# Token-shift features of a two-block layer: gelu output written at the commonest shift, seven shift copies per chunk for twelve, and a new written-out order

## The chip, the cores and the metric

The kernel runs on one core of a Trainium2 chip. The metric is the device time of one execution in microseconds (us); "before" has a median of 192.87 us over 6 runs (192.69 to 193.13). A core has five instruction streams that the kernel fills: TensorE (PE, matrix products; its weight loads are shown as PEld), VectorE (DVE), ScalarE (ACT), GpSimd (POOL) and SyncE (SP), which here only issues DMA transfers. Each takes its instructions strictly in order; they wait for each other through semaphores.

## The reference

The input x is 2048 rows of 448 features; weights and data are bf16.

```python
# A: attention block, 16 heads of 28 features, 8 keys at distance 0, 2, ... 14 rows back
qkv = (layernorm(x) @ wqkv)
attn = softmax(q . k * 28**-0.5 over the 8 keys, keys before row 0 masked)
h = x + (attn @ v) @ wo
# B: token shift and MLP, c = 112
y = layernorm(h)                              # B's own input
g = gelu(layernorm(y) @ w1)
g0 = rows of g[:, 0:112]   moved down by 1    # row s takes row s-1, row 0 takes zeros
g1 = rows of g[:, 112:224] moved up by 1      # row s takes row s+1
g2 = rows of g[:, 224:336] moved down by 2
g3 = rows of g[:, 336:448] moved up by 2
x1 = y + concat(g0, g1, g2, g3) @ w2
out = h + x1 + gelu(layernorm(x1) @ w3) @ w4  # w3 448x1792, w4 1792x448
```

## The kernel before

**Tiling.** The rows are cut into 4 chunks (c = 0 to 3) of 512. Inside a chunk even rows (p = 0) and odd rows (p = 1) are kept apart, 256 each, so that a shift by an even number of rows stays in its half and a shift by one row changes the half. A tile is 128 rows of one parity, and there are 16 of them (`NTL`). Features lie on partitions for the products: 448 features are read as four windows of 128 (`windows`).

**Operations.** `_fast_path` builds a list of operations, each with a tag, an engine, and the operations that it depends on. The tags, which this text uses as names (c a chunk, g a group of tiles):

- A1_c: layer norm of x, statistics on DVE, the factors on POOL, the normalised tiles `lntm` on ACT or DVE, and the transposes into `hT`: by PE for chunks 0 and 1 (four 128x128 transposes per tile into PSUM, then a copy to `hT` on ACT or DVE), by DMA from SP for chunks 2 and 3, one per tile (tr2_0 to tr2_3, tr3_0 to tr3_3).
- V_c, QK_c: products with wqkv; their .e0 to .e3 copy PSUM to `vt` and `qk`, on ACT or DVE.
- S_c.p, E_c.p, AV_c.p: scores (p is one of two groups of heads), exponential on ACT with a mask product on DVE, and the product with v. N_c is the division by the softmax sum, for chunks 2 and 3 with transfers through DRAM (zg, zs, zb).
- WO_c: product with wo; its .e0 and .e1 add x on DVE.
- B1_c, X_c, W1_c: layer norms of B (transposed by one DMA, tr1, tr2 or tr0, into `actT`), and the product with w1, whose .e0 and .e1 are the gelus.
- G_c: the shift copies. W2_g: the product with w2. L3_g, W3_g, W4_g: layer norm, w3 with gelu, w4. W2 to W4 work on groups of tiles (`GROUPS`: 2, 4, 4, 4 and 2), since a chunk's last rows need the next chunk's features.

**Shifts.** Each of the four feature groups has 112 features: 64 (window 0 of the gelu result `gA`), 32 and 16. Features 0 to 63 of all groups sit in `gA`, in two windows, one for each parity, and the shift there is only a choice of columns in `g_rows`. The remaining 48 features per group are packed in three 128-partition slots: two slots with the 32-feature blocks (both parities), one slot with 16-feature blocks, in which both parities stand on different partitions. The gelu .e1 writes these 768 columns to `gtm` (128x768), and G_c copies them from there to `gB` (four copies of 32x512) and `gC` (eight copies of 32x256 and 16x256) at the wanted shift. In the last chunk three small memsets fill columns at the end. `shift` lets a copy run on ACT or DVE, as the order says. `w1_p` is w1 with its columns repacked to make the features come out on those partitions, and `w2_s` is w2 with its rows in the same order; `load_attn_out` does both.

**What sets the order.** Nothing is decided at run time. `_ORDER` is a written table of operation numbers. A letter behind a number (a, v, p) chooses ACT, DVE or POOL, and digits behind a colon name PSUM banks. `schedule` fills the engines' queues in that order, `_emit_plan` adds the semaphore waits, `emit` (L1390) issues them; most instructions carry L1407, so tiles' names tell them apart. The figures `occ` and `lat` in the code describe durations to the program that wrote the table; they reach the chip only through it.

**Start.** PE first runs `WARM` products on zeros. `START` is the offset in instructions, within blocks of 256, at which PE's stream begins.

**Loads.** All weights are loaded by SP: wqkv first, then w1, w2 and wo. The w3 halves (w300, w301, w310, w311, 448 KB each) and w4 (w40 to w43) follow in four or more places in the middle. Each has no dependency, so its place in SP's queue alone decides when it starts.

Of the kernel before, what the change touches and what calls it, by code (L numbers as in the profile page):

```python
# [228 lines left out]
WARM = 14  # L229
LATE = 2  # L230

START = 128
# [3 lines left out]
2 1 4 3 7 6 8 5 12 17 0 16 13 15 45 65 74 64 67 68 79 21 19 18:7 22 20 28 23 24 25 26 29 27 35 30 32 36:7 33:6  # L236
31 38 39:5 37a 41 34a 42:7 40v 43v 51:40 52 53 14 59 84 82 48v 156 47v 9 10 50a 62 63 80 49a 46a 78 69 134 132
72 73 138 136 135 139 133 137 11 178 142 54 180 85:62 71 86 87 88 184 205 185 140 182 70 179 98 99 101 103 102
113 109 111 110 106 107 104 112 108 105 57a 141 56a 97 89a 100 91:40 90a 92 220:26 93 201 181 143 221 223 144v
153v 150v 183 94 145:3 146a 147v 55:2 95a 96v 151:7 154:6 58v 148:3 152v 149v 203 76 75 77 222 224 188 155a  # L240
234:40 186 187 166:62 237 238 123p 167 168 204 60 235 236 61 225:54 198 165 115a 230 226 231 227 232 228 233 229
170a 169 171a 172:60 189 196a 173 174 175 197 239:54 161:3 240 244 241 245 242 246 243 247 66 130 190a 191 176a
177a 164a 346:06 382 192a 193 199 200 206 202 207 209 81 349 347 194v 157:42 158 159 117p 119v 160 348 208 162a
248:06 249 250 350 163a 360:24 252 251 361 254 253 210 213a 378:1 351:32 381a 363 362 255 356 260 364 256 121a
258 257 259 261 195 264 215a 389:60 352 390 214 118a 391 211a 217a 393a 262 365:54 370 366 371 367 372 368 369
218 263 392 394a 353 265 269v 267v 124 357 266a 383:26 354 535:04 538 373 536 219 384 385 386 355 388a 358 114p
268v 359 537 374:04 375 376 120v 387a 377 128 539 379a 116p 380a 528:26 416:04 529 417 270 418 531 419 540:6 530
216 532 126 420 421 403 424 122p 428 426 422 425 429 427 423 279:02 430 432 212 541a 543 125 431 280 281 282
533:6 283 534v 284 433 434v 437v 293a 294a 295a 439 436v 129 286v 288v 291v 292v 289v 440 404:04 435a 287a 405
406 407 296a 409a 542 408a 438 290a 273 271 272 274 544 441 395:62 396 397 398 285v 401v 400a 276v 278v 275v  # L250
277v 297:04 298 299 300 301 302 303 304 305 306 442 545 443a 549 446v 546 447:26 448 449 451 307 308 309 310 450
452 456v 459v 463v 454v 461a 457a 453v 462v 460a 458a 464a 445v 410:40 411 412 414a 455v 547 413 548 415v 131
312v 399:7 311v 402a 552 465:24 551 666:60 313 550 466 467 553 667 469 669 468 470 473 554:60 555 556 558 477
474 478 316:42 317 318 557 319 475 559 44 320 471 476 472 560 127 562 566 563 564 561 322:46 323 324 325 567 565
481 479 480 482 570 568 569 571 484v 579 483v 321 486v 328:02 577 578 314 329 330 331 327 326 334:46 335 670 332
336 333 668 338 337 485a 315 673:02 572v 340:5 487 339 343:7 676 574v 575a 573v 576 671:2 341 674 677 675 678:0
344 672v 489 490 492:64 493 494 488 495 491 680 679a 681 682 683 684 685 687 497 496 342 686 580 583v 585:02 586
587 588 589 590 599v 600a 595v 596v 592a 498:64 591v 594v 499 500 501 601a 593v 503 504:20 505 506 507 602a 597v
598v 581v 502 508 444v 603:64 604 605 607 83 609 611 509 610 688 510:02 511 512 513 689 612 606 608 691 613 514
615 690 616 614 515 617 516:7 519:6 692:42 693 694 695 517 520 618 518 619 620 623v 624v 621v 622a 625 627 521  # L260
697 696 704 698 700 701 699 705 702 703 706 707 708 525:7 744 522:6 629 745 526 523 709 713a 642:42 643 644 710v
712a 711v 524 714 717 626 527 645 584v 630:60 631 632 633 647 715 716 718 646 635 634 636:42 637 582v 638 640
746 639 641 723:60 724 725 648:24 649 650 727 652 726 728 722v 719v 732a 720v 736v 733v 735a 739v 730v 741a 734
731v 729v 742 738a 743a 740v 651 653 737 654:7 812:02 813 814 721v 815 655 816 817 820 345 818 821 819 749:64
750 751 752 824 753 754 757 656 755 758 822 823 825 756 759 761 762 760 765 747:3 628 663:2 763 764 660:7 826a
827a 828 664 766 748 661 662 770a 769v 768v 767v 657:6 849:24 850 851 852 771 658 831:60 832 833 854 853 835
837:24 834 836 838 839 840 843:06 844 845 842 841 829 846 848 830 847 782:24 783 784 788:06 786 785 787 789 790
791 792 793 665 776:42 777 778 780 794:60 795 796 797 779 781 799 858:5 659 774 806:4 855:3 859 856 857 860 798
772 775 800:7 807 773 801 802 808 803:6 809:7 804 805 810 811
""".split()  # L270


def _fast_path(nc, es, flag, A_x, A_wqkv, A_wo, B_w1, B_w2, B_w3, B_w4, out):
    SEQ, D = A_x.shape[1], A_x.shape[2]
# [14 lines left out]
    def sb(name, shape, dt):  # L289
        return es.enter_context(nc.sbuf_tensor(name, shape, dt))  # L290
# [1208 lines left out]
```

## Time and profile before

| | |
|---|---|
| median of 6 runs | 192.87 us |
| profiled execution | 193.29 us, span 191.6 us, granted clock 1.00 |
| PE's first warm-up product, first V_0 product | 2.58 us, 8.46 us |
| first statistics on DVE | 3.62 us |
| AV_2.0 starts | 59.73 us |
| S_3.0 starts, W3_0 starts | 77.68 us, 82.85 us |
| instruction transfers (queue q8) | 25 of 16 KB |

The span runs from the first instruction of the profiled execution to the last. The page gives, for each engine, its busy time; then the chain that ended last (each piece followed back to what released it), the costliest groups of instructions (busy time and mean duration in ns, then the idle time ahead of the group and who ended it), and the DMA queues. An idle time attributed to "issue" is one for which the profile shows no producer. A timeline row gives start, length, engine, operation, tiles and count, and in brackets the idle time ahead. DMA rows for a stretch give queue and kind, packets, MB, and time taken as a share of the stretch times 16 transfer engines.

### The profile page before, as it was taken

How to read it: one execution, taken by the hardware profiler on the slowest of the kernel's cores; microseconds unless marked ns; L12 is line 12 of the kernel's file. 1: busy time of each engine (PE TensorE's matmuls, PEld its weight loads, DVE VectorE, ACT ScalarE, POOL GpSimd, SP SyncE). 2: the span in 40 equal slices, each digit the busy share in tenths (PEclk: the TensorE clock that was granted, in tenths of full speed). 3: DMA queues.
4: the chain of work that ended last, by engine and by line, in shares of the span. 5: the costliest groups of instructions: out<-in, count | busy, mean ns of one | idle time of the engine just before them, and what ended most of it. 6: DMA issues, size and time to landing. Idle time of an engine off the chain costs nothing.

```text
span 191.6 us, 6790 instructions
## 1 busy us (share of the span) xinstructions
PE 183.1 (96%) x2999; PEld 102.3 (53%) x2999; DVE 128.8 (67%) x313; ACT 112.1 (59%) x149; POOL 41.3 (22%) x101
## 2 busy tenths in 40 slices
PE   7999999998897999999999999999999999999994
PEld 2445556554555564577556464444566568454551
DVE  7899988999985779999773379794038970001241
ACT  2769899597849749938758930117782326564000
POOL 3147400507104603005910002143000320000000
DMA  5975307437297766620653600507000133000021
GB/s 141 337 241 139 94 12 153 34 33 145 92 144 217 196 159 151 71 88 0 113 119 91 163 3 0 129 28 182 2 0 27 41 98 104 3 0 3 3 99 51
DMA packets 32479, 17.77 MB, mean 93 GB/s; under 512 B 22524, under 2 KB 31932, under 8 KB 32444
## 3 DMA queue, kind: packets, MB, share of 16 engines
q1 hardware_dynamic: 32156, 17.05, 37.8%
q8 instruction: 25, 0.41, 0.9%
q10 hardware_dynamic: 288, 0.23, 0.4%
q14 instruction: 10, 0.08, 0.2%
HBM read 10.07 MB, written 1.90 MB: 62 GB/s over the span
## 4 chain that ended last, share of the span: by engine, by line
PE 78%; ACT 9%; DVE 8%; POOL 2%; DMA 1%; issue 1%
PE ps L1407 78%; DVE st L1407 3%; ACT gC L1407 2%; POOL rstd L1407 2%; DMA xin<-in_A_x_dram 1%; ACT gtm L1407 1%; DVE xin L1407 1%; ACT gA L1407 1%; ACT qk L1407 1%; ACT pt L1407 1%; ACT vt L1407 1%; DVE qk L1407 1%; DVE lntm L1407 1%; DVE xb L1407 1%; DVE mv L1407 1%
## 5 line engine op out<-in xcount | busy, mean ns | idle before, releaser
L1407 PE MATMUL ps<-actT,w_s 64*128 64x512 bf16 (+2 forms) x560 | 44.2, 312 | 0.0
L1407 PE MATMUL ps<-w_s,arena 128*128 128x448 bf16 x224 | 43.4, 353 | 0.0
L1407 DVE TENSOR_TENSOR xb<-ps,xb 128x448 bf16<-128x448 f32 (+1 forms) x26 | 18.4, 724 | 32.8 <-PE ps L1407 32.7
L1407 ACT ACTIVATE arena<-ps 128x512 bf16<-128x512 f32 (+2 forms) x40 | 29.0, 767 | 16.9 <-PE ps L1407 16.6
L1407 PEld LDWEIGHTS ps<-actT,w_s 64*128 64x128 bf16 x560 | 26.3, 94 | 16.9 <-DVE xb L1407 0.4
L1407 PEld LDWEIGHTS ps<-w_s,arena 128*128 128x128 bf16 x224 | 21.4, 98 | 20.8 <-ACT arena L1407 0.6
L1407 PE MATMUL ps<-hT,arena 64*128 64x512 bf16 x224 | 25.7, 377 | 0.1
L1407 POOL TENSOR_TENSOR rstd<-vtmp,mhalf 128x4 f32<-128x4 f32 (+1 forms) x16 | 18.4, 1153 | 1.1
L1407 DVE BATCH_NORM_STATS2 st<-xin 128x6 f32<-128x448 bf16 x32 | 18.1, 605 | 0.2 <-DMA xin<-in_A_x_dram 0.2
L1407 ACT ACTIVATE pt<-ps 128x1024 bf16<-128x1024 f32 x16 | 15.7, 1021 | 3.6 <-PE ps L1407 3.5
L1407 PEld LDWEIGHTS ps<-hT,arena 64*128 64x128 bf16 x224 | 10.8, 94 | 11.6 <-ACT qk L1407 0.4
L1407 ACT ACTIVATE qk<-ps 128x1024 bf16<-128x1024 f32 x14 | 13.9, 1021 | 2.9 <-PE ps L1407 2.8
L1407 ACT ACTIVATE lntm<-xin,nmr,rstd 128x512 bf16<-128x512 bf16 x13 | 10.2, 808 | 8.8 <-POOL nmr L1407 8.3
L1407 PE MATMUL ps<-arena,hT 64*64 64x448 bf16 (+1 forms) x248 | 15.1, 352 | 0.2 <-DVE hT L1407 0.2
L1407 POOL TENSOR_SCALAR vtmp<-mv 128x4 f32<-128x4 f32 (+1 forms) x16 | 3.4, 215 | 50.0 <-DVE mv L1407 49.2
L1407 PE MATMUL ps<-wo_s,oT 64*128 64x448 bf16 x128 | 13.1, 350 | 0.6 <-ACT vt L1407 0.5
L1407 POOL TENSOR_SCALAR nmr<-mv 128x4 f32<-128x4 f32 (+1 forms) x16 | 4.3, 272 | 41.9 <-DVE mv L1407 41.8
L1407 PE MATMUL ps<-actT,w_p 64*128 64x512 bf16 (+1 forms) x140 | 13.0, 333 | 0.0
L1407 ACT ACTIVATE lntm<-xb,nmr,rstd 128x512 bf16<-128x512 bf16 x5 | 4.0, 812 | 15.1 <-POOL nmr L1407 15.1
L1407 DVE COPY gC<-gtm 32x256 bf16<-32x256 bf16 (+1 forms) x15 | 3.4, 228 | 13.3 <-ACT gtm L1407 12.9
L1407 DVE TENSOR_TENSOR pt<-pt,msk 128x1024 bf16<-128x1024 bf16 x16 | 10.5, 683 | 0.7 <-ACT pt L1407 0.7
L1407 PEld LDWEIGHTS ps<-actT,w_p 64*128 64x128 bf16 x140 | 8.4, 94 | 3.9
(90 smaller groups left out, 226.3 us busy)
## 6 DMA issues: line engine op xcount, KB each, us to landing
w_s<-in_B_w_dram SPq DMA_DIRECT2D x6, 448.0 KB, 4.2
rzb<-rz_scratch SPq DMA_DIRECT2D x8, 256.0 KB, 4.4
out_dram<-xb SPq DMA_DIRECT2D x16, 112.0 KB, 2.1
xin<-in_A_x_dram SPq DMA_DIRECT2D x3, 448.0 KB, 7.2
arena<-in_A_wqkv_dram SPq DMA_DIRECT2D x2, 448.0 KB, 5.6
w_s<-in_B_w_dram SPq DMA_DIRECT2D x2, 336.0 KB, 5.1
arena<-in_A_wqkv_dram SPq DMA_DIRECT2D x2, 224.0 KB, 4.9
w_s<-in_B_w_dram SPq DMA_DIRECT2D x2, 224.0 KB, 3.6
```

The lines of the kernel that those rows point to most:

```text
L1407: inst = getattr(eng, meth)(**kw)
```

## The change

Three things are changed.

*The shift copies.* `gtm`, `gB` and `gC` become one tile `gBC` of four slots (128 partitions, 4 x (HALF+4) columns). The gelu .e1 writes slots 0 to 2 directly at an offset of 2, so a feature whose shift is the one that this offset gives needs no copy. Of the two 32-feature slots only partitions 32 to 63 (by 1) and 96 to 127 (by 2) are moved, in place, to the left. Slot 3 is a moved image of slot 2: a copy of all 128 partitions, then four copies of 32 or 16 partitions over parts of it. That is seven copies per chunk, and no memsets in the last one. The 16-feature blocks are put on other partitions (the constants in `load_attn_out`, for `w2_s` and `w1_p`), so that blocks of one shift lie side by side.

*The order.* `_ORDER` is new throughout, with other engine letters. PE's operations keep nearly the same sequence. The numbers of operations change by one to six, as there are fewer of them. Of the places spoken of below: the four copies that empty the first transposes (A1_0) run on ACT, ACT, DVE, DVE (tiles 1, 0, 2, 3) before, and tiles 0 and 2 on ACT, 1 and 3 on DVE after; the normalise for tr2_0 moves behind V_1's evictions on ACT; in SP's queue, w300 and w40 before V_2, then tr2, tr3_2, w310, tr3_0, zg1, w301, w41 become w40, tr3_2, tr2, tr3_1, tr3_0, w301, w300, w41, zg1, and w310 and w311 stand behind the zb transfers of chunk 2. The engines of the shift copies after (ACT + DVE) are 2 + 5, 2 + 5, 1 + 6 and 2 + 5 for chunks 0 to 3.

*Small constants.* One warm-up product fewer, another start offset (128 becomes 132), wv loaded ahead of wqk, and figures in the cost model, which act only through the order.

```diff
-WARM = 14
+WARM = 13
 LATE = 2
-START = 128
+START = 132
 _ORDER = """
...
-31 38 39:5 37a 41 34a 42:7 40v 43v 51:40 52 53 14 59 84 82 48v 156 47v 9 10 50a 62 63 80 49a 46a 78 69 134 132
...
+2 17 1 59 3 4 5 6 8 7 82 0 64 16 12 21 15 19 22 20 28 23 24 25 26 13 67 68 18:7 29 35 27 30 36:7 32 31 33:6 34a
+38 14 41 9 10 11 39:5 37v 42:4 43v 79 111 69 40a 65 50a 49v 48v 47a 72 74 155 45 46v 78 133 135 51:60 131 137 52
...
-    gB = sb("gB", [128, 2, HALF + 4], BF16)
-    gC = sb("gC", [128, HALF + 4], BF16)
-    gtm = sb("gtm", [128, 2, 768], BF16)
+    gBC = sb("gBC", [128, 4, HALF + 4], BF16)
...
-    win_load("wqk", wqk_s, A_wqkv[:, 0:2 * D], 512 * 2 * D * 2, ("sp", "sp"))
-    win_load("wv", wv_s, A_wqkv[:, 2 * D:3 * D], 512 * D * 2, ("sp", "sp"))
+    win_load("wv", wv_s, A_wqkv[:, 2 * D:3 * D], 512 * D * 2, ("sp", "sp"), 190.0)
+    win_load("wqk", wqk_s, A_wqkv[:, 0:2 * D], 512 * 2 * D * 2, ("sp", "sp"), 280.0)
...
-        pool("memset", 140, ap=gB[:, :, 0:2], constant=0.0)
-        pool("memset", 140, ap=gB[:, :, HALF:HALF + 2], constant=0.0)
-        pool("memset", 140, ap=gC[:, 0:2], constant=0.0)
+        pool("memset", 140, ap=gBC[:, :, 0:2], constant=0.0)
+        pool("memset", 140, ap=gBC[:, :, HALF + 2:HALF + 4], constant=0.0)
...
-                k = 64 * h + 32 * (g // 2) + 16 * (1 - g % 2)
+                k = ((32, 0, 48, 16), (64, 112, 80, 96))[h][g]
...
-            for g, o in ((x, 384), (2 + x, 480), (2 + x, 544), (x, 576)):
-                o += 16 * (1 - x)
+            for g, o in (((0, 416), (2, 464), (2, 560), (0, 576)), ((1, 384), (3, 480), (3, 528), (1, 624)))[x]:
...
         tag("W1_%d.e1" % c)
-        gt = gtm[:, c % 2, :]
-        act(gt, T2(lambda p: p.rearrange("k u n -> k (u n)")[:, 0:768]), ACT.Gelu_apprx_tanh, 768)
+        o = 2 + 256 * c
+        act(gBC[:, 0:3, o:o + 256], T2(lambda p: p.rearrange("k u n -> k (u n)")[:, 0:768].rearrange("k (t n) -> k t n", t=3)),
+            ACT.Gelu_apprx_tanh, 768)
         tag("G_%d" % c)
-        for q, sh in enumerate((0, -1, 0, -2)):
-            r = slice(32 * q, 32 * q + 32)
-            o = 2 + 256 * c + sh
-            shift(gB[r, :, o:o + 256], gt[r, 0:512].rearrange("k (p n) -> k p n", p=2), 512)
-        for q, (s1, s2) in enumerate(((-1, 0), (-1, 1), (0, 1), (-1, 1))):
-            for m, sh in ((32, s2), (16, s1)):
-                r = slice(32 * q, 32 * q + m)
-                o = 1 + 256 * c + sh
-                shift(gC[r, o:o + 256], gt[r, 512:768], 256)
-                if c == NCH - 1 and m == 32 and s1 < 0:
-                    dve("memset", 145, ap=gC[32 * q:32 * q + 16, HALF:HALF + 1], constant=0.0)
+        last = c == NCH - 1
+        for r0, m, d, e in ((32, 32, 1, 1), (96, 32, 2, 2)):
+            v = gBC[r0:r0 + m, 0:2, :]
+            shift(v[:, :, o - d:o - d + 256 + e * last], v[:, :, o:o + 256 + e * last], 512)
+        for r0, m, d, e in ((0, 128, 0, 0), (0, 32, 2, 1), (32, 16, 1, 0), (96, 32, 1, 0), (96, 16, 2, 1)):
+            v = gBC[r0:r0 + m, :, :]
+            shift(v[:, 3, o - d:o - d + 256 + e * last], v[:, 2, o:o + 256 + e * last], 256)
...
-            return gB[r, q, n + o:n + o + 128]
-        return gC[r, n + 1:n + 129]
+            return gBC[r, q, n + o:n + o + 128]
+        return gBC[r, 3, n + 1:n + 129]
```

## Prediction

> **What bounds the kernel now.** I read the page first, then the chain of waits, PE's waits, and the timelines and DMA rows around the waits.
>
> ```profile
> PE 183.1 (96%) x2999; PEld 102.3 (53%) x2999; DVE 128.8 (67%) x313; ACT 112.1 (59%) x149; POOL 41.3 (22%) x101
> ...
> PE 78%; ACT 9%; DVE 8%; POOL 2%; DMA 1%; issue 1%
> ```
>
> PE is busy 183.1 of 191.6 us and carries 78% of the chain; the changed kernel gives it the same matmuls in nearly the same order. So the change can only open or close PE's waits. Two lie behind the shift copies. The first, in the chain's pieces (start, length, what):
>
> ```profile
> 72.82 0.70 ACT gtm L1407
> ...
> 73.54 0.41 ACT gC L1407
> ...
> 75.30 0.41 ACT gC L1407
> ...
> 75.74 1.03 ACT qk L1407
> ...
> 76.82 1.18 PE ps L1407 x38
> ```
>
> From 73.54 to 75.72 ACT does five copies one after another; only then can it empty the PSUM of QK_3, for which PE waits until 76.82. The second, in the same view, before W2_4:
>
> ```profile
> 140.90 0.82 ACT gtm L1407
> ...
> 141.74 0.63 ACT gB L1407
> ...
> 143.71 0.42 ACT gC L1407
> ...
> 144.26 2.82 PE ps L1407 x41
> ```
>
> Third, PE's waits (total, times, longest), and its timeline at the longest that no producer explains:
>
> ```profile
> PE ps L1407 <- issue: 1.6, 3, 1.1
> ```
>
> ```profile
> 59.73 0.76 PE L1407 MATMUL ps<-pt,vt 64*32 64x52 bf16 x75
> 61.60 0.21 PE L1407 MATMUL ps<-pt,vt 64*32 64x51 bf16 x5 [1.10 <-issue]
> ```
>
> In AV_2.0 PE stops 1.3 us (start to start, less the usual spacing) inside one operation, with all inputs there. The trace has a DMA queue of kind "instruction" whose packets are 16 KB, 25 in all; counting PE's instructions, all three "issue" stops fall where such a block ends. The DMA rows of two stretches show when those packets come:
>
> ```profile
> q1 hardware_dynamic: 739, 0.86, 90.7%
> ```
>
> ```profile
> q1 hardware_dynamic: 48, 0.03, 7.3%
> q8 instruction: 1, 0.02, 5.5%
> ```
>
> PE crosses a block's end at 46.13. From 46.1 to 48.8 (first fence) two weight loads move and no instruction packet does; it comes in 48.8 to 50.1 (second), once they are through. It is the same before AV_2.0: crossing at 56.26, load w310 issued at 55.21 and landed at 59.25, packet at 59.27, PE running again at 61.60, 2.3 us after the packet began. Where only a small transpose is in flight (crossing 42.72) the packet comes at 43.86, 1.14 us after.
>
> **The change part by part.** Times are those of before; a minus is a gain.
>
> (1) *Fewer copies.* Rows by form:
>
> ```profile
> L1407 ACT ACTIVATE gC<-gtm 16x256 bf16<-16x256 bf16 x11 | 4.6, 414 | 0.5 <-DVE gC L1407 0.3
> ...
> L1407 DVE COPY gB<-gtm 32x512 bf16<-32x512 bf16 x13 | 3.6, 280 | 0.4
> ...
> L1407 ACT ACTIVATE gC<-gtm 32x256 bf16<-32x256 bf16 x6 | 2.5, 414 | 0.2
> L1407 DVE COPY gC<-gtm 32x256 bf16<-32x256 bf16 x10 | 2.2, 224 | 13.2 <-ACT gtm L1407 12.9
> ...
> L1407 ACT ACTIVATE gB<-gtm 32x512 bf16<-32x512 bf16 x3 | 1.9, 629 | 0.1
> ```
>
> 16 and 32 rows cost the same (414 ns), so rows do not matter and the new 128-row copy is taken at the same 414 (ACT) or 224 (DVE). ACT: 20 copies of 9.0 us become 7 of 5x0.414+2x0.629 = 3.3. DVE: 28 copies and 3 memsets, 7.2 us, become 21 copies, 6x0.28+15x0.224 = 5.0. The gelu keeps 768 elements, 802 ns. Nearly all of that is beside PE's work; only two places are on the path.
>
> *Before W2_1.* ACT runs gelu e1 (0.70), e0 (1.03), two copies (0.83) and QK_3.e2 (1.03) for gelus, five copies (2.2) and QK_3.e2: about 1.3 us less. PE stood from 76.10 to 76.82; ACT ends well before that, so the wait of 0.72 closes. By PE's own durations W2_1 is due at 76.22 and starts 0.05 after its releaser: -0.55. Bounds -0.72 and 0 (DVE's five copies, of which three are a chain on one tile, 3x0.224 plus hand-offs, come last instead).
>
> *Before W2_4.* ACT after 140.90: gelu 0.82, then two 629 ns copies, ending 143.0 for 144.12; DVE's five, from 141.72, end near 143. PE is ready at 143.76 and waited 0.50: -0.4. Bounds -0.5 and 0. Late next: W3 of the group before, whose PSUM the same ACT empties at 144.14; it too comes earlier.
>
> (2) *The order of the loads and AV_2.0.* Before, SP issues w300 and w40 at 43.94 and 45.20, w310 at 55.21. In the new order SP holds only w40 in the forties; w301, w300 and w41 stand behind the transpose tr3_0, which waits for an ACT normalise placed after the exponentials of E_2.0 (ACT 54.43): normalise to 55.2, tr3_0's issue 1.2, so w301 issues at 56.5 to 57.0. Its data flow some 2.5 us after issue, as w310's did (55.21, full rate from about 57.8). PE crosses at 56.3 to 56.7; with only a transpose in flight, the packet comes 1.14 later, 57.4 to 57.8, ahead of w301's data at 59.0, and is usable 2.3 later, near 60.0. PE reaches the block's end at 60.3. I take the stop as gone: -1.2. Bounds -1.3 and 0. Queued on SP behind these three loads are zg1 (57.88 before, 59.5 at worst; what reads it comes after zg0 at 63.12), zg0 and tr1, which has 64.13 to wait for. w310 and w311 now issue behind the four zb reads, near 70, where w43 did (69.86, landed 76.45); W3_0's later groups, from about 85, read them. The block that PE needs at 78.09 came at 72.16 there, so it has 3.6 us of cover.
>
> [...]
>
> (3) *The head.* Of the four copies that empty the first transposes, the third moves from DVE (0.42) to ACT (0.60), and a small memset (0.06) enters DVE's first statistics. V_0 starts 8.67 for 8.46: +0.2. Bounds 0 and +0.4 (two 0.2 hand-offs). One warm-up matmul fewer costs nothing: PE waits for the first normalised tile (6.66) anyway. Loading wv ahead of wqk: wv is early, wqk's pads end by 10.5 against QK_0's 11.4 and hide it.
>
> (4) *tr2_0.* The last transpose for QK_2.2 now hangs on an ACT normalise behind V_1's two evictions (35.12), ending 35.9 to 36.6; before, the last one was on DVE and ended at 34.63, landing 38.77. Single transposes here landed 2.5 to 4.1 us after their normalise: 39.1 to 40.7, and QK_2.2 is due at 39.7. Wait 0 to 1.0; I take 0.65, the middle. 0.35 of it comes back, since AV_1.1, just behind, stops 0.42 at a block's end and would then find the block there: +0.3. Bounds 0 and +1.0.
>
> (5) *Small moves.* E_3.0's exponentials come earlier (PE waits 0.23 at WO_2: -0.05) and masks too (0.26 at AV_3.1: -0.15): -0.2, bounds -0.4 and 0. The order moves some 150 other operations; I walked each queue past its neighbours and found slack (W1_1's tr1 lands 0.5 to 1 us early, the least; if gone, that much). The PSUM waits, the two-block rows of w1 and w2 and the tail from 188.7 cost nothing: same count, same forms, under PE's work.
>
> Sum: -0.55 -0.4 -1.2 +0.2 +0.3 -0.2 = -1.85. The profiled execution was 193.29 (span 191.6 and 1.7 around it), 0.42 over the median of 192.87; it would be 191.4, the median 191.0. All best ends together give -0.72-0.5-1.3-0.4 = -2.9 (190.0); all worst +0.4+1.0 = +1.4 (194.3).
>
> **The rivals.**
>
> *The block's fetch is late all the same* (AV_2.0 keeps its stop). For: tr3_0 is still in flight at the crossing, and before it was too. Against: 42.72, with only a transpose, was prompt. Then -0.65: 192.2.
>
> *The copies' time is hidden anyway*: DVE's chained copies or a table load end where ACT's did, parts W2_1 and W2_4 give nothing, and the stop stays: +0.2+0.3-0.2 = +0.3, 193.2. Against: three chained DVE copies are 0.7 us, five of ACT's were 2.1.
>
> *Slower: a load catches the fetch.* Three loads now go out together, 1344 KB, at the 380 GB/s seen in the forties 3.5 us. If their data flow before the packet is asked for, it comes near 62.5, usable 64.8, a stop of 3.9 for 1.3: -0.65+2.6, 194.8. The same with w40, now first (issue near 43.3, data from 45.8) and the crossing of AV_1.1: S_2.1 would stop 3.0 for 0.5, giving -1.85+2.5 = +0.65, 193.5. It decides when w301 issues over 1.4 us ahead of PE's crossing (I have it 0 to 0.7 behind), or w40 over 1.4 ahead (I have it 0.2 to 0.6 behind). A transpose tr2_0 later than any row here works the same way by delaying PE.
>
> **How the numbers follow.** Forecast case 0.52 (190.4 to 191.7: steps 3 and 4 at either end); stop stays 0.20 (191.8 to 192.6); hidden 0.10 (192.6 to 193.2); slower 0.18 (193.5 to 194.8, and what of 150 moved operations I misread). A difference under 0.2%, 0.39 us, can't be told from none. Faster: 0.52 and nearly all of 0.20, 0.70; same 0.11; slower 0.19. The range 190.3 to 193.6 leaves out some 0.04 below and 0.13 above.
>
> **What would show it.** AV_2.0 without an "issue" wait, and an instruction packet near 57.5: step 2 right. W2_1 and W2_4 in the chain without ACT copies ahead of them: step 1. PE's first V_0 near 8.7: step 3. A PE wait on DMA hT near 40: step 4, wrong if over 1 us. The prediction fails if an "issue" wait of 2 us or more stands anywhere, or a new wait over 0.5 us on a DMA or on DVE's gBC.

## The result, and the profile after

| | before | after |
|---|---|---|
| median, all executions | 192.90 us (71) | 193.29 us (34) |
| lowest and highest | 191.78, 193.99 us | 191.57, 196.62 us |
| profiled execution, its span | 193.29, 191.6 us | 191.84, 190.1 us |

The ratio of after to before is 0.9993, with a 95% interval of 0.998 to 1.0006; it leaves out executions more than 1.5% above the shortest of their kernel, which are ten of the 34 of after and none of before, while the medians and extremes here leave out nothing. So the change gained nothing that can be measured, where 191.0 us had been forecast.

Two things stand out in the table. The profiled execution took 191.84 us, close to the 191.4 that the sum gave for it. And the changed kernel's executions differ by 5 us among themselves, those of before by 2.2. The forecast was of one path through the work, and one value cannot stand for such a spread. The page of after, busy times and the chain's shares:

```profile
PE 182.5 (96%) x2998; PEld 103.9 (55%) x2998; DVE 123.0 (65%) x294; ACT 110.8 (58%) x141; POOL 40.6 (21%) x104
...
PE 81%; ACT 8%; DVE 6%; POOL 2%; DMA 2%; issue 1%
```

PE does the same work (182.5 us for 183.1); DVE has 5.8 us less of it, ACT 1.3. The groups of instructions on the new tile of after show the copies (count, then durations in ns, least, median and most, then first and last start and the forms):

```profile
L1401 DVE COPY gBC<-gBC x21: 215/227/293, 62.8 to 141.8; 16x256 bf16<-16x256 bf16 x6, 32x512 bf16<-32x512 bf16 x6, 32x256 bf16<-32x256 bf16 x4, 128x256 bf16<-128x256 bf16 x3
L1401 ACT ACTIVATE gBC<-gBC x7: 412/414/631, 62.3 to 141.4; 32x256 bf16<-32x256 bf16 x3, 128x256 bf16<-128x256 bf16 x1, 16x256 bf16<-16x256 bf16 x1, 32x516 bf16<-32x516 bf16 x1
L1401 ACT ACTIVATE gBC<-ps x4: 802/809/812, 60.9 to 139.9; 128x768 bf16<-128x768 f32 x4
```

So 28 copies stand where 48 stood, at the durations assumed. PE's timeline of after, at AV_2.0, WO_2, AV_3.1 and W1_2:

```profile
59.13 0.81 PE L1401 MATMUL ps<-pt,vt 64*32 64x52 bf16 x80
...
78.38 2.45 PE L1401 MATMUL ps<-wo_s,oT 64*128 64x448 bf16 x24 [0.36 <-ACT pt L1401]
...
94.54 0.90 PE L1401 MATMUL ps<-pt,vt 64*32 64x52 bf16 x80 [0.27 <-DVE pt L1401]
...
98.78 3.21 PE L1401 MATMUL ps<-actT,w_p 64*128 64x512 bf16 x35 [0.21 <-issue]
```

AV_2.0's 80 products run in one piece; in the profile of before they stood in two rows with 1.10 us of "issue" between them. And three waits are there that before had smaller or not at all. The chain of waits of after, 71 to 79 us, leads to the first of them:

```profile
70.93 3.49 PE ps L1401 x32
...
74.44 0.54 ACT vt L1401
...
75.00 1.28 ACT L1401
...
76.30 1.95 ACT pt L1401 x2
...
78.38 0.72 PE ps L1401 x5
```

No shift copy is left in it: ACT's vt copy, the load of an activation table (the piece of 1.28 us, ACT_TABLE_LOAD in the timeline), and the two exponentials that follow the scores at 75.19 now set when WO_2 may start. ACT stood idle for 0.23 us ahead of the vt copy, waiting for V_3's products, so fewer copies can't start this chain earlier. Comparing the starts of the same PE operations in the two profiles (after less before, in us) gives the whole path:

| PE operation | before | after | difference so far | step |
|---|---|---|---|---|
| V_0 | 8.46 | 8.79 | +0.33 | +0.33, head |
| scores behind WO_0's first products | 36.22 | 36.18 | -0.04 | -0.37 in small pieces |
| product behind AV_1.1 | 43.11 | 42.71 | -0.40 | -0.36, block end |
| product behind S_2.1 | 46.28 | 45.67 | -0.61 | -0.21, block end |
| AV_2.0 | 59.73 | 59.13 | -0.60 | 0 |
| product behind AV_2.0 | 61.94 | 60.05 | -1.89 | -1.29, block end |
| W2_1 | 76.82 | 74.33 | -2.49 | -0.60, copies |
| WO_2 | 80.58 | 78.38 | -2.20 | +0.29 |
| AV_3.0 | 95.42 | 93.47 | -1.95 | +0.25 |
| behind AV_3.1 | 97.07 | 95.37 | -1.70 | +0.25 |
| W1_2 | 100.10 | 98.78 | -1.32 | +0.38 |
| W2_4 | 144.26 | 142.56 | -1.70 | -0.38, copies |
| last W4 | 172.65 | 171.06 | -1.59 | +0.11 |

In this execution the expected gains are there and 1.17 us is given back behind W2_1. Another 0.9 us of gain (0.37, 0.36 and 0.21 in the second to fourth rows) was forecast as none, or as a loss. What differs from execution to execution, and what takes the rest, needed experiments.

### The profile page after: what moved, and what is told of

The parts are those of the page before. It is cut to its first block, busy times and chain, and to the rows that moved or that the text cites. A ratio compares the mean times of both kernels' runs of the same rounds, so it can differ in the third digit from the quotient of the medians.

```text
span 190.1 us, 6765 instructions
## 1 busy us (share of the span) xinstructions
PE 182.5 (96%) x2998; PEld 103.9 (55%) x2998; DVE 123.0 (65%) x294; ACT 110.8 (58%) x141; POOL 40.6 (21%) x104
## 4 chain that ended last, share of the span: by engine, by line
PE 81%; ACT 8%; DVE 6%; POOL 2%; DMA 2%; issue 1%
PE ps L1401 81%; ACT qk L1401 2%; ACT pt L1401 2%; DVE st L1401 2%; DMA xin<-in_A_x_dram 2%; ACT L1401 1%; POOL rstd L1401 1%; ACT vt L1401 1%; DVE lntm L1401 1%; DVE xb L1401 1%; DVE pt L1401 1%; ACT hT L1401 1%; DVE xin L1401 1%; DVE mv L1401 1%; ACT lntm L1401 0%
## 5 line engine op out<-in xcount | busy, mean ns | idle before, releaser
L1401 PEld LDWEIGHTS ps<-actT,w_s 64*128 64x128 bf16 x560 | 28.1, 94 | 15.3 <-issue 0.6
L1401 POOL TENSOR_TENSOR rstd<-vtmp,mhalf 128x4 f32<-128x4 f32 (+1 forms) x16 | 17.5, 1096 | 1.0
L1401 ACT ACTIVATE lntm<-xin,nmr,rstd 128x512 bf16<-128x512 bf16 x14 | 11.2, 812 | 10.0 <-POOL gBC L1401 7.9
L1401 DVE COPY gBC<-gBC 16x256 bf16<-16x256 bf16 (+5 forms) x21 | 5.0, 244 | 15.5 <-ACT gBC L1401 15.0
L1401 PEld LDWEIGHTS ps<-arena,hT 64*64 64x64 bf16 (+1 forms) x248 | 7.3, 107 | 6.1 <-ACT gBC L1401 0.8
```

The source lines that it names most:

```text
L1401: inst = getattr(eng, meth)(**kw)
```

## The experiments

Theory A: the time at PE's block ends is a race. In before, the 16 KB packet of the "instruction" queue came 1.14 us after PE crossed a block's end where only a small transpose was in flight (42.72, 43.86), and 3.01 us after it where w310 was (56.26, 59.27); the theory is that the packet waits for a load which already flows. The new order leaves hundredths of a microsecond of margin, so the gain of AV_2.0 is won in some executions and lost in others. Theory B (rival): the fetches are harmless, and the gain of the copies is spent on later waits that the new order makes. Theory C (rival, formed after the first runs): something ahead of AV_2.0 varies, and PE's fetch only shows it. Ratios are to before on the same chip, with 95% intervals. (The recorded expectations use other letters: their theory F is A here, and their rival C is any other source of the spread, such as the clock, the transposes or the order itself.)

### 1. The same kernel again, and loads moved near the crossing

**The changed kernel, unchanged** (no edit).

> The changed kernel, unchanged, to see its spread. Theory F (a weight load catches the fetch of PE's next instruction block, in some executions only, since w301 goes out 0.07 us behind PE's crossing of a block's end at 55.70): times from 191.5 to above 195, and whenever the profiled execution is above 193 it has an 'issue' wait of PE of 1.5 us or more in AV_2.0, or at another block's end, with the instruction packet later than its neighbours. Rival C (the spread comes from the granted clock or from the landing of the transposes): a profiled execution above 193 shows its loss spread over the stages or at waits on DMA, and the instruction packets at their places.

Measured: 193.17 us (192.36 to 194.02), ratio 1.0011 (0.9981 to 1.0042); its profiled execution took 194.02 us. Here one program has two profiles, 191.84 and 194.02 us. PE's waits of the second run, then its timeline:

```profile
PE ps L1401 <- issue: 2.1, 4, 1.4
```

```profile
45.73 0.22 PE L1401 MATMUL ps<-qk 28*64 28x51 bf16 x5 [0.24 <-issue]
...
56.29 0.26 PE L1401 MATMUL ps<-pt,vt 64*32 64x51 bf16 x18 [0.25 <-issue]
...
61.76 0.21 PE L1401 MATMUL ps<-pt,vt 64*32 64x51 bf16 x6 [1.39 <-issue]
```

The first profile has 0.2 us of "issue" in all. The three timeline rows begin at the 2177th, 2689th and 2944th of PE's instructions, which lie two blocks and one block of 256 apart, to within one. SP's row for w301, w300 and w41 in the first profile, and then in the second:

```profile
55.77 3.42 SPq L1401 DMA_DIRECT2D w_s<-in_B_w_dram  x3
```

```profile
55.99 1.61 SPq L1401 DMA_DIRECT2D w_s<-in_B_w_dram  x3
```

Counting PE's instructions, PE crosses the block's end ahead of AV_2.0 at 55.80 in the first, 0.03 us after the loads begin to issue (the expectation had them the other way round, by 0.07). In the second a small stop (0.25 us, second timeline row) puts the crossing at 56.29, 0.30 us after them. The transfers of the first profile from 57.0 to 59.2:

```profile
q1 hardware_dynamic: 332, 0.57, 87.3%
q8 instruction: 1, 0.02, 5.6%
```

and of the second, first from 56.2 to 59.3, with no instruction packet in it, then from 59.3 to 60.4:

```profile
q1 hardware_dynamic: 715, 0.63, 75.9%
```

```profile
q1 hardware_dynamic: 274, 0.41, 98.2%
q8 instruction: 1, 0.02, 5.4%
```

The packet came 1.25 us after the crossing (57.05) in one and 3.05 us (59.34) in the other, and in the second PE stood 1.39 us in AV_2.0. So 0.27 us more of lead for the loads goes with a stop of 1.39. The granted clock of the second execution is 1.00, so the clock is not what makes it longer.

**Loads ahead of tr3_0, to force the late fetch.**

```diff
-426 427 213 210a 80 397 211 124 529:4 123 218 428v 530a 128 431v
+426 427 213 124 123 128 210a 80 397 211 529:4 218 428v 530a 431v
```

(In the order of after, 123 to 126 are w300, w301, w310, w311, and 127 to 130 are w40 to w43.)

> The changed kernel with w301, w300 and w41 taken ahead of tr3_0, so that they go out about 53.2 to 54.5, 1.2 us or more before PE's crossing at 55.7. Theory F: every execution has the late fetch: packet after 58.5, a stop in AV_2.0 of 1.5 to 4 us, median 194 to 196. Rival C: no change against the changed kernel, 193.3, or a wait for tr3_0 before QK_3.0 of under 1 us.

Measured: 195.0 us (193.83 to 198.3, 4 executions), ratio 1.0086 (1.0048 to 1.0123). SP's row and PE's in AV_2.0 of this run:

```profile
53.79 2.22 SPq L1401 DMA_DIRECT2D w_s<-in_B_w_dram  x3
```

```profile
63.19 0.21 PE L1401 MATMUL ps<-pt,vt 64*32 64x51 bf16 x6 [2.76 <-issue]
```

With the loads 2.56 us ahead of the crossing (56.35), the packet came 4.61 us after it and the stop grew to 2.76. The same three loads, earlier, cost 1.4 to 2.8 us more at this one place: theory A in its direction.

**Loads behind zb, to clear the crossing** (w41 behind w311).

```diff
-397 211 124 529:4 123 218 428v 530a 128 431v
+397 211 529:4 218 428v 530a 431v
...
-389:64 390 391 536 403a
+389:64 390 391 536 124 123 403a
...
-125 452a 126 303
+125 452a 126 128 303
```

> The changed kernel with the three loads w301, w300 and w41 taken from behind tr3_0 (55.8) to behind the zb transfers (about 69.5), beside w310 and w311; all else the same. Theory F: no load is in flight when PE asks for the block at 55.7, the slow executions go, all times lie between 191.3 and 192.6 with a median near 191.8, 1.1 us below the kernel before. Rival C: median near 193.3 with the same spread up to 196.

Measured: 194.62 us (193.58 to 195.97), ratio 1.009 (1.005 to 1.013). AV_2.0 does not stop, and still the kernel is slower. SP and PE of this run:

```profile
69.06 3.57 SPq L1401 DMA_DIRECT2D w_s<-in_B_w_dram  x5
73.87 4.43 SPq L1401 DMA_TRANSPOSE actT<-lntm  x1
```

```profile
82.75 1.71 PE L1401 MATMUL ps<-actT,w_s 64*128 64x256 bf16 x28 [1.73 <-DVE st L1401]
```

Five loads together put tr0 behind them; its issue took 4.43 us, and W3_0 waited 1.73. The 1.29 of AV_2.0 was bought with a dearer wait.

**Loads split, behind tr1 and behind w43.**

```diff
-397 211 124 529:4 123 218 428v 530a 128 431v
+397 211 529:4 218 428v 530a 431v
...
-286a 288v 432 287v
+286a 288v 432 124 123 287v
...
-467 315 130 463
+467 315 130 128 463
```

> The changed kernel with w301 and w300 behind the transpose tr1 (64.5 in place of 55.8) and w41 behind w43 (75.5). The earlier move of all three behind the zb transfers took the stop in AV_2.0 away but held up tr0 behind five loads, and W3_0 waited 1.73 us. Theory F: no load is in flight at PE's crossing of 55.7, tr0 goes out at 73.7 as in the changed kernel, no wait over 0.6 us on PE; median 191.8, all within 191.3 to 192.6. Rival C (the spread has another source): median 193.3, runs up to 196.

Measured: 193.69 us (192.63 to 195.55, 12 executions), ratio 1.0049 (1.0026 to 1.0071). AV_2.0 runs through again; the price is elsewhere:

```profile
71.62 1.74 SPq L1401 DMA_DIRECT2D rzb<-rz_scratch  x4
```

```profile
80.76 2.44 PE L1401 MATMUL ps<-wo_s,oT 64*128 64x448 bf16 x24 [1.62 <-DVE oT L1401]
```

The zb reads issue at 71.62 where after has 67.07, since what writes the data for them was held up by the two loads, and WO_2 waits 1.62 for the division. Another 0.69 us is a wait of AV_0.0 on POOL, where nothing was changed; that was the first sign of theory C.

### 2. The kernel before, with one load moved, and the copies alone

**Before, with w310 behind w43.** Numbers are those of before (126 is w310, 131 is w43).

```diff
-530 216 532 126 420 421
+530 216 532 420 421
...
-548 415v 131 312v
+548 415v 131 126 312v
```

> The kernel before with one load, w310, taken from ahead of tr3_0 (55.21) to behind w43 (70.3). Theory F: the packet comes about 1.2 us after the crossing at 56.26 in place of 3.0, AV_2.0's stop of 1.3 us goes, median 191.7. Rival C, and the reading that the stop is no matter of the loads: 192.9 and the stop stays.

Measured: 192.0 us (191.51 to 192.46), ratio 0.9948 (0.9923 to 0.9972). PE's waits and AV_2.0:

```profile
PE ps L1407 <- issue: 0.3, 1, 0.3
```

```profile
59.45 0.81 PE L1407 MATMUL ps<-pt,vt 64*32 64x52 bf16 x80
```

The packet came 1.0 us after the crossing, and 1.6 us of "issue" fell to 0.3. One load moved in the old kernel is worth 1.0 us, with no other change: the stop is real time and it is the load that makes it. B can't explain this.

**The new copies in the old order and with the old loads.**

```diff
-    gB = sb("gB", [128, 2, HALF + 4], BF16)
-    gC = sb("gC", [128, HALF + 4], BF16)
-    gtm = sb("gtm", [128, 2, 768], BF16)
+    gBC = sb("gBC", [128, 4, HALF + 4], BF16)
...
+        act(gBC[:, 0:3, o:o + 256], T2(lambda p: p.rearrange("k u n -> k (u n)")[:, 0:768].rearrange("k (t n) -> k t n", t=3)),
...
+        for k in range(5):
+            S.add_many("flex", [], 0, 0).opts = {"dve": [], "act": []}
...
 _ORDER = """
...
-533:6 283 534v 284 433 434v 437v 293a 294a 295a 439 436v
+533:6 283 534v 284 433 434v 437v 287a 289v 288v 439 436v
...
```

(Empty operations keep the old numbers; the 16-feature blocks and the loop of seven copies are those of the change; the copies' places in G_0 to G_3 hold the seven.)

> Part 1 alone: the kernel before with its own order, loads and start, but the gelu into the four-slot tile and seven copies per chunk, on the engines that the changed kernel uses; the twelve copies' other places in the table are left empty. If the steps on W2_1 (-0.55) and W2_4 (-0.4) are right: median 191.9, no ACT copy ahead of W2_1 or W2_4 in PE's waits, and AV_2.0's stop of 1.3 us still there with the packet at about 59. If the copies are hidden anyway: 192.9.

Measured: 192.34 us (192.03 to 194.07, 12 executions), against 192.61 of before on this chip; ratio 0.9995 (0.9974 to 1.0016). W2_1 gained 0.59 and W2_4 0.38, as in after, and then WO_2 took back 0.20 and the way from there to W1_2 another 0.50, 0.39 of it at W1_2 itself. AV_2.0, WO_2 and W1_2 of this run:

```profile
60.26 0.60 PE L1405 MATMUL ps<-pt,vt 64*32 64x52 bf16 x37 [0.70 <-issue]
...
79.24 2.44 PE L1405 MATMUL ps<-wo_s,oT 64*128 64x448 bf16 x24 [0.27 <-ACT pt L1405]
...
99.26 3.21 PE L1405 MATMUL ps<-actT,w_p 64*128 64x512 bf16 x35 [0.23 <-DMA actT<-lntm]
```

The stop in AV_2.0 falls 63 instructions ahead of the block's end here, not at it as in the other three runs with a stop there; why is not shown.

The chain ahead of W1_2:

```profile
88.95 2.90 POOL rstd L1405
...
92.48 0.73 DVE lntm L1405 x2
...
93.24 5.89 DMA actT<-lntm
...
99.26 0.80 PE ps L1405 x5
```

So the copies alone are worth what the page of before said at their own two places, and 0.7 of their 0.97 us goes to waits further on. That part of B holds, for the copies: the next transpose of B1_2 hangs on POOL's 2.90 us and its own 5.89, which did not move when PE did.

**The copies and the late w310 together** (the kernel just above, with the edit of the one above that).

```diff
-530 216 532 126 420 421
+530 216 532 420 421
...
-548 415v 131 312v
+548 415v 131 126 312v
```

> The former kernel (part 1 alone) with one more edit: w310 behind w43, which by itself brought the kernel before to 192.0. Theory F and additive steps: 190.9 to 191.2, with a spread under 1 us, faster than both kernels. If the copies are hidden: 192.0.

Measured: 191.92 us (191.31 to 192.31, 12 executions), ratio 0.9961 (0.9947 to 0.9975), span 190.5. Its executions differ by 1.0 us where after's differ by 5. On top of the late w310 the copies add nothing that these runs can tell.

**The same with POOL's slow operation freed.** R_0 and E_3.0's mask products (314, 670, 668 and 315 in this order) stand behind B1_2's normalises.

```diff
-328:02 577 578 314 329 330 331 327 326 334:46 335 670 332
-336 333 668 338 337 485a 315 673:02 572v
+328:02 577 578 329 330 331 327 326 334:46 335 332
+336 333 338 337 485a 673:02 572v
...
-574v 575a 573v 576 671:2
+574v 575a 573v 314 670 668 315 576 671:2
```

> Part 1 alone with w310 late, and one edit on DVE: the two mask products of E_3.0 and the two sums R_0 move behind the three normalises of B1_2. In the kernels so far the power operation of B1_2 on POOL took 2.90 us while DVE ran those products, against 1.04 in B1_1, and DVE then stood idle 1.2 us for it. If the copies' gain is given back at W1_2 through that chain (power operation, normalise, transpose tr0): the power operation takes 2.0 or less, tr0 goes out 1 us earlier, W1_2's wait on it goes, and the median falls 0.5 below the former 191.92, to 191.4. If W1_2 is held by something else: 191.9, or slower by up to 0.5 because the masks now end too late for AV_3.0.

Measured: 191.42 us (190.94 to 192.04, 8 executions), ratio 0.9933 (0.9909 to 0.9957), span 189.8. The power in rstd before this edit, and after it:

```profile
88.69 2.89 POOL L1405 TENSOR_TENSOR rstd<-vtmp,mhalf 128x4 f32<-128x4 f32 x1
```

```profile
88.70 1.08 POOL L1405 TENSOR_TENSOR rstd<-vtmp,mhalf 128x4 f32<-128x4 f32 x1
```

With R_0 and E_3.0's mask products away from it the same instruction takes 1.08 us, W1_2 no longer waits, and the median is 0.5 us lower (on another chip, and the two ratios' intervals overlap a little). This kernel is faster than both the one before and the one after.

### 3. The block ends from the other side

**Another start offset in PE's instruction blocks.**

```diff
-START = 132
+START = 232
```

> The changed kernel with START 232 for 132 and nothing else: no load, no transpose and no operation moves, only the ends of PE's instruction blocks fall 100 instructions earlier, so the crossing at 55.7 comes at about 55.2, ahead of w301's issue by 0.6 us, and that at 51.1 ahead of tr2's data. Theory F: the packet is asked for ahead of the loads in every execution; median 191.2 to 192.0, no 'issue' wait over 0.5 us in AV_2.0. If the loads slow PE by something other than the fetch (Rival C), the time and its spread stay: 193.3.

Measured: 198.6 us (195.66 to 202.33, 6 executions), ratio 1.0224 (1.0166 to 1.0281). Nothing but the places of the block ends has changed, and the kernel is 5 us slower. The expectation missed: it followed the block ends at 51.1 and 55.7, and all the others moved with them. The stops are now elsewhere (25.37, 33.34), the longest in AV_3.1:

```profile
100.24 0.21 PE L1401 MATMUL ps<-pt,vt 64*32 64x51 bf16 x2 [2.30 <-issue]
```

The busy times of this run in two stretches (length, then PE, PEld, DVE, ACT, POOL with counts, granted clock, DMA share, GB/s):

```profile
98.00:102.00 4.00, 1.76 (x10) 0.67 (x11) 1.22 (x1) 1.19 (x1) 0.00 (x0) 0.79 0.71 60
102.00:116.00 14.00, 14.00 (x133) 6.94 (x131) 3.89 (x13) 8.60 (x10) 0.00 (x0) 0.94 0.37 88
```

This stop is followed by a lower granted clock: 0.79 over the first stretch, and then 0.94 over 14 us of full work; the 28 products behind the stop take 4.81 us, for 3.20 in the first profile of after. So here the stop costs more than its length. It is no rule of these runs: after the longer stop with the loads ahead of tr3_0 (2.76 us) the clock is 1.00 in every stretch. The three stops make 3.0 of the 6.2 us by which this span is longer than that of the first profile of after; a wait of 1.27 us for DVE's masks at 42.30 is new too, and not explained.

### 4. What else varies in the changed kernel

**The changed kernel on the chip of the next two, as their control** (no edit).

> The changed kernel unchanged, on the same chip as the next three, as their yardstick: median 193.2, spread from 191.6 to over 194.5. Its profiled execution is either without a stop in AV_2.0 (span about 190.1) or with one of 1.3 us or more (span about 192.3 or longer); both have the copies' waits before W2_1 and W2_4 gone.

Measured: 193.34 us (191.49 to 194.96, 12 executions), ratio 1.0018 (0.9988 to 1.0049); profiled 192.31.

**All five loads out of the way** (w300, w301, w41 behind zb; w310, w311 behind w43).

```diff
-397 211 124 529:4 123 218 428v 530a 128 431v
+397 211 529:4 218 428v 530a 431v
...
-390 391 536 403a
+390 391 536 124 123 128 403a
...
-448v 125 452a 126 303
+448v 452a 303
...
-467 315 130 463
+467 315 130 125 126 463
```

> The changed kernel with w301, w300 and w41 behind the zb transfers (69 us), and w310 and w311 behind w43 (76 us): no load near the crossings at 51 to 60, and, unlike the two earlier tries, at most three loads ahead of tr0 and none ahead of zs0. Theory F (the loads make the late fetches): median 191.7, all between 191.2 and 192.6. Rival C (the spread is in the new order itself): median 193, runs up to 195.

Measured: 193.05 us (191.35 to 195.33, 12 executions), ratio 1.0002 (0.9976 to 1.0028). Its profiled execution, 191.35 us, has a span of 189.6 and no stop; the spread of the others is as wide as before. Clearing AV_2.0's crossing does not by itself narrow the kernel: A alone is too small.

**The loads as before has them** (w300 behind w40, w301 and w41 behind zg1, w311 behind tr0).

```diff
-265a 127 524:20
+265a 127 123 524:20
...
-397 211 124 529:4 123 218 428v 530a 128 431v
+397 211 529:4 218 428v 530a 431v
...
-522:4 532 282
+522:4 532 124 128 282
...
-452a 126 303
+452a 303
...
-458 307 459
+458 307 126 459
```

> The changed kernel with its loads at the places which gave the kernel before 192.0 and a spread of 1 us: w40 and w300 in the forties, w301 and w41 behind zg1, w310 behind zb, w311 behind tr0. Theory F: median 191.7, spread about 1 us, no stop over 0.5 us in AV_2.0. Rival C: 193, spread of 3 us. If the small stop at AV_2.1 (0.2 to 0.45, from tr2 in flight at the crossing of 51.1) is what sets the spread, it stays and the median is 192.3.

Measured: 192.31 us (191.44 to 193.25, 12 executions), ratio 0.9983 (0.996 to 1.0005). That is 1.0 us under the control in the median, and the spread is halved. This is the new order and the new copies with the old grouping of loads.

**The changed kernel, two single executions** (no edit).

> The changed kernel unchanged, one execution with its profile, whichever it is. By the theory of late fetches and POOL copies, its time is 191.8 plus the sum of PE's waits that the fastest profile does not have: 0.75 if POOL's copy is late at AV_0.0, 0.2 to 0.45 at AV_2.1, 1.4 to 4 at AV_2.0, and nothing over 0.3 us elsewhere.

> The same as the former, a second execution: 191.8 plus the waits at AV_0.0, AV_2.1 and AV_2.0, nothing over 0.3 us elsewhere.

Measured: 192.79 and 193.15 us. Neither stops in AV_2.0; both wait in AV_0.0 instead. POOL's timeline in the first profile of after, then POOL, DVE and PE in the first of these two:

```profile
22.72 0.38 POOL L1401 COPY w_p<-w_s 128x64 bf16<-128x64 bf16 x1
23.03 0.97 POOL L1401 MEMSET vt<- 128x240 bf16 x2
```

```profile
22.19 2.28 POOL L1401 COPY w_p<-w_s 128x64 bf16<-128x64 bf16 x1
24.41 0.95 POOL L1401 MEMSET vt<- 128x240 bf16 x2
```

```profile
21.90 2.48 DVE L1401 TENSOR_TENSOR pt<-pt,msk 128x1024 bf16<-128x1024 bf16 x4
```

```profile
25.50 0.68 PE L1401 MATMUL ps<-pt,vt 64*32 64x52 bf16 x66 [1.42 <-POOL hT L1401]
```

The same small copy of w1 takes 0.38 or 2.28 us. In both it falls beside DVE's four mask products. In the first profile those begin at 22.07, just after the larger copy of w1 ahead of it (21.84), and it is they that take longer, 2.82 us for 2.48; here they begin at 21.90, 0.29 us ahead of the small copy, and it is POOL that is held up. In the repeat the copy begins 0.43 us behind them and takes 0.36. So the overlap alone does not decide, and these runs do not show what does. In the new order it stands ahead of the last memsets of `vt`, which AV_0.0 needs; in before these memsets are done by 21.2. The profile names the last POOL tile (hT), but the two rows above it are what is late. AV_0.0 waits 1.42 us here, 0.84 in the second, 0.88 in the control, and nothing in the first profile and the repeat. That is theory C, and in a single execution it is worth as much as AV_2.0's stop.

Of POOL's instructions the small copy here and the power of section 2 are held up (0.38 to 2.28, 1.08 to 2.89), and the two memsets of `vt` are not: 0.97 beside DVE's mask products in the first profile, 0.95 behind them here. POOL is held up for longer than one DVE instruction lasts (its 2.28 us against 2.48 for four of them).

**POOL's two copies behind the memsets.**

```diff
-55:2 146v 114p 152v
+55:2 146v 152v
...
-95v 62 120p 129
+95v 62 129
...
-60 221 61 223
+60 221 61 114p 120p 223
```

> The changed kernel with two POOL copies of w1 (ops 114 and 120, which wait for w1 to land) moved behind the memsets of vt that AV_0.0 needs, where they stood before the change; all else the same. In two of the eleven profiled executions of the new order so far one of those copies took 1.7 us in place of 0.24 to 0.38, beside DVE's mask products, the memsets came 0.8 us later and PE waited 0.75 us at AV_0.0. If this and the late fetch before AV_2.0 together make the spread: no wait at AV_0.0, the time falls by 0.75 in a fifth of the executions only, median 193.0, and the runs above 194.5 stay. If the POOL copies were the main source: median 192.2 and a spread of 1.5.

Measured: 193.95 us (191.47 to 195.71, 12 executions), ratio 1.0006 (0.9967 to 1.0045); profiled 194.09. AV_0.0 does not wait, and PE stops at the next block's end:

```profile
27.79 2.33 PE L1401 MATMUL ps<-hT,arena 64*128 64x512 bf16 x20 [1.35 <-issue]
```

PE crosses at 21.32, the packet comes 4.11 us after the crossing, and QK_1.2 stops for 1.35. In this execution the wait was taken away and another of the same size came in its place. The load nearest to it is w42, which the new order has ahead of the tr2 transposes and before had behind them. But w42 issues 0.64 us behind the crossing here, and 0.33 behind it in the first profile, where the packet came after 1.10; so its lead does not decide, and what held this packet is not shown.

**Both: POOL's copies behind the memsets and the loads as before.**

```diff
-55:2 146v 114p 152v
+55:2 146v 152v
...
-60 221 61 223
+60 221 61 114p 120p 223
...
-397 211 124 529:4 123 218 428v 530a 128 431v
+397 211 529:4 218 428v 530a 431v
...
```

> The former edit together with the loads at the places that gave the changed kernel 192.31 (w40 and w300 in the forties, w301 and w41 behind zg1, w310 behind zb, w311 behind tr0). If late fetches and the POOL copies make the spread between them: median 192.0 to 192.2, all within 191.4 to 192.9. If something else does: 192.3 with runs above 193, as without the POOL edit.

Measured: 192.1 us (191.59 to 192.82, 12 executions), ratio 0.9954 (0.9929 to 0.9978). Apart they gave 0.9983 and 1.0006, with intervals that hold 1; together they are faster than before and spread over 1.2 us. The kernel above differs from this one by the loads alone, on the same chip, and has a median 1.85 us higher; the same loads alone gave 1.0 us above. So it is mainly the old places of the loads that bring the median down. What POOL's copies add to that these runs can't tell (0.9954 with them, 0.9983 without, on two chips).

**And w42 behind tr2_3.**

```diff
-62 129 153:4
+62 153:4
...
-168 196 118p
+168 196 129 118p
```

> The changed kernel with the POOL order and the load places of the last version, and one more load, w42, moved from ahead of the transpose tr2_3 (22.0, just behind PE's crossing at 21.4) to behind it, where it stood before the change. In one profiled execution of the new order the packet asked for at 21.39 came 4.1 us later and PE stopped 1.35 us in QK_1.2. If w42 makes that: no stop there, packet at +1 to 2; median 191.9 to 192.1, highest run under 192.7. If not: as without the edit, 192.1 with runs to 192.9.

Measured: 192.52 us (191.82 to 192.68, 12 executions), ratio 0.9961 (0.9945 to 0.9977). QK_1.2 does not stop, but it did not in the profile of the kernel above either, with the packet 1.2 us after the crossing; and in the median the two can't be told apart. So this run does not show that w42 makes the stop.

**And E_3.0's masks and R_0 behind B1_2's normalises.**

```diff
-475v 654 557 558 657:20 308 334:5 333 474a 652 559
+475v 557 558 657:20 334:5 333 474a 559
...
-337:7 561v 335
+337:7 561v 654 308 652 335
```

> The former kernel with the two masks of E_3.0 and one sum R_0 on DVE moved behind the three normalises of B1_2, as in the version of the old order that gave 191.42. If the new order gives part of its gain back at W1_2 for the same reason (the power operation on POOL 2.56 us beside the masks): that operation takes 2.0 or less, tr0 goes out 0.6 to 1.0 earlier, and the median is 0.4 below the former kernel's, 191.5 to 191.7. If the masks are then late for AV_3.0 and AV_3.1: no gain.

Measured: 191.82 us (191.32 to 191.98, 6 executions), ratio 0.993 (0.9909 to 0.9951), span 190.2 for 190.9. The power without and with the edit:

```profile
89.35 2.56 POOL L1401 TENSOR_TENSOR rstd<-vtmp,mhalf 128x4 f32<-128x4 f32 x1
```

```profile
89.18 1.05 POOL L1401 TENSOR_TENSOR rstd<-vtmp,mhalf 128x4 f32<-128x4 f32 x1
```

The changed kernel with four groups of operations moved is 0.7% faster than before, as the old order with the copies, the late w310 and the masks is (0.9933). What was given back at W1_2 comes back here too. The new order shows no gain over the old one so mended.

Counting PE's instructions in all profiled executions but that with START at 232, PE crosses the block's end ahead of AV_2.0 nineteen times. In four a load had been issued 0.30 to 2.56 us ahead of the crossing (0.30 in the repeat, 0.76 with the copies alone, 1.04 in before, 2.56 with the loads forced ahead): the packet came 2.8 to 4.6 us after it, and AV_2.0 stopped for 0.70 to 2.76 us. SP's row for w310 in before, where PE crosses at 56.26:

```profile
55.21 0.59 SPq L1407 DMA_DIRECT2D w_s<-in_B_w_dram  x1
```

In the other fifteen the next loads were issued at most 0.03 us ahead of the crossing, or behind it: the packet came 1.0 to 1.75 us after it, and no such stop followed. Of the five profiled executions of the changed kernel only the repeat had the late packet.

## Why the prediction was wrong

The forecast was a gain of 1.85 us, about 1%, and the runs show none. By its own steps, with the first profile's numbers where nothing else is said:

- **(1) Copies: right in size, wrong in what it leaves.** -0.55 and -0.4 were forecast, -0.60 and -0.38 were measured, the same in the kernel with the copies alone. What failed is "late next". The prediction looked for it at W3 of the group before; it was WO_2 (+0.29, ACT's table load and exponentials behind V_3) and W1_2 (+0.38, POOL's power and a transpose), which hang on chains that don't start any earlier when the copies go.
- **(2) The order of the loads: the step that failed.** -1.2 was forecast and -1.29 is what a good execution shows, but the step gave one value to a race. The forecast put w301's issue 0 to 0.7 us behind PE's crossing, and its rival asked for 1.4 us ahead of it to decide. The runs had it 0.03 us ahead (no stop) and 0.30 ahead (stop of 1.39), so the point from which the rival decides lies between these, not at 1.4. The prediction's own rows spoke against 1.4: in before w310 is issued 1.04 us ahead of the crossing (55.21, 56.26), and its packet is late. The rival's price was right in kind (2.76 us where the loads are forced ahead, for 3.9 forecast) and its place was missed by over a microsecond. What the step rests on holds: where the packet was late PE stopped for 0.70 to 2.76 us in AV_2.0, and moving one load in the old kernel gained 1.0 us.
- **(3) The head:** +0.33 for +0.2, inside its bounds.
- **(4) tr2_0:** -0.36 for +0.3. The wait for tr2_0 did not come, QK_2.2 starts in time in the first profile, and AV_1.1's block end gives back 0.36.
- **(5) Small moves: the other step that failed.** -0.2 was forecast and +0.79 was found at WO_2, AV_3.0 and AV_3.1, with W1_2's +0.38 to 1.17 in all. The sentence that each queue had been "walked past its neighbours" and had slack was wrong there, and at one place more: POOL's copies of w1, now ahead of the memsets of `vt` (0.69 to 1.42 us at AV_0.0 in the executions where DVE's products hold them up). That depends on what runs beside them, which a walk with fixed durations does not show.

So the sum of -1.85 became -1.5 in an execution in which everything falls well. That it came so near is in part luck, since 0.9 us of gain that was not forecast (0.37 and 0.21 in no step, 0.36 against a loss in step 4) made up for most of the 1.17 given back. The other four profiled executions of the changed kernel lose time at AV_2.0 or at AV_0.0, 2.1 us of "issue" in the repeat and 0.84 to 1.42 at AV_0.0 in the other three. That is what is seen of the lost gain; half of the 34 executions took longer than 193.29 us, and of executions that long only the repeat (194.02) was profiled, so the account of the median is not complete. Of the prediction's signs of failure, a new wait over 0.5 us did come; it was expected on a DMA or on DVE's gBC, and was on POOL.

Not settled: the longest executions of after (195 to 196.6 us) and of the kernel with all five loads moved (195.33) were not among the profiled ones, so where they lose is not shown. Three of the ten longest (195.29, 196.48 and 196.62 us) list a granted clock of 0.99, as the run with START at 232 does, the others 1.00. Why the old grouping of the loads narrows the spread, and moving all five far back does not, is open with it.

## What to carry to other kernels

Before a wait is booked as gone, find the margin that decides it (here under 0.3 us), and what moves it: a gain that hangs on a race is worth its odds, and the time of one profile is one draw. Where stops with no producer lie multiples of 256 of PE's instructions apart (the 2177th, 2689th and 2944th here, to within one), look at which loads are in flight at the block's end, and move the load, not PE's work (w310 alone was worth 1.0 us). When a path is shortened, price the next consumer of the same chain, and look for POOL instructions on it that run beside DVE's mask products (2.89 us for 1.08 here).

## What the runs showed of the hardware

- At the block's end ahead of AV_2.0 the packet came 1.0 to 1.75 us after PE's crossing in the fifteen profiled executions whose next weight loads were issued at most 0.03 us ahead of it, and 2.8 to 4.6 us after it in the four where one was issued 0.30 us or more ahead; where PE had stopped at a block's end it went on 2.2 to 2.8 us after the packet. Moving the block ends by 100 instructions alone cost 5 us.
- POOL's small copy of w1 and its power in rstd could take 2.4 to 6 times as long beside DVE's mask products: 2.28 for 0.38 us (copy), 2.89 for 1.08 and 2.56 for 1.05 (power). In the first profile the copy took 0.38 beside them, and they took 2.82 for 2.48.
- After a stop of 2.30 us the granted clock was 0.79 over the 4 us around it and 0.94 over the 14 us that followed; after one of 2.76 us in another run it stayed at 1.00.
